# Threshold attention and a feed-forward block: raw weight chunks with other limits, fewer begun behind the turning, additions behind the thresholds

## The chip, the core and the metric

One Trainium2 chip, of which the kernel uses one core. The metric is the device time of one execution in microseconds, lower is better. Profile times are counted from the first instruction of one profiled execution.

## What is computed

```python
def _attn_ref(q, k, v, tau):                       # q, k, v: (8, 8, 576, 64)
    scores = scale * np.matmul(q, k.transpose(0, 1, 3, 2))
    thresh = np.max(scores, axis=-1, keepdims=True) - tau
    scores = np.where(scores >= thresh, scores, -1000000000.0)
    scores = scores - np.max(scores, axis=-1, keepdims=True)
    attn = np.exp(scores)
    attn = attn / (np.sum(attn, axis=-1, keepdims=True) + 1e-09)
    return np.matmul(attn, v)

def _moe_ref(x, g_ln, w_ch1, w_ch2):               # x: (8, 576, 512), heads side by side
    mu = np.mean(x, axis=-1, keepdims=True)
    var = np.mean((x - mu) ** 2, axis=-1, keepdims=True)
    xn = (x - mu) / np.sqrt(var + 1e-06) * g_ln
    return x + np.maximum(xn @ w_ch1, 0.0) @ w_ch2
```

`w_ch1` (512 x 2048) and `w_ch2` (2048 x 512) come in as 64-bit floats. The kernel sees them as 64-bit integers and makes 32-bit floats of them itself.

## The kernel before

**Slots.** The attention of one batch is cut into nine slots (`SLOTS = 9`), 72 in all. A slot takes two heads and half of their rows, or, in the fifth, the remaining rows of all heads. In the main loop, a slot `n` goes through these steps: `scores` (L402) on TensorE; `exponentials`, with the row maximum (L416) on VectorE, the threshold (L420) on GpSimd and the exponential (L429) on ScalarE; `weights`, which masks and sums (L436) on VectorE and divides by the sum (L452) on GpSimd; and the turning of the weights. From slot 6 on (`FIRST = 6`), the turning is `turn_blocks` (L520, L526): VectorE transposes blocks into `et`, a DMA writes `et` to a scratch in DRAM (`scr`), and in the next slot `fetch` reads it back as `em` and `er`. The products with v (`values_of`, L595 and L605) then run at the end of the next slot. Each slot has four quarters, at whose ends `second_part(n, i)` gives TensorE a share of the feed-forward work.

**The feed-forward.** It is done in sixteen groups of 288 tokens. Group 0 begins in slot 6, group 1 in the middle of slot 10. `first_part` makes 64 products with `w_ch1`, each followed after four by a Relu on ScalarE (L793) into `hidden`. Group 0 (`plain`) then makes 64 products with `w_ch2` in `second_plain`; later groups use `second_quarters`. A product of 288 columns is four records in the trace. Two PSUM banks (`ps_ff`) take turns, so a product can wait for the Relu that frees its bank. The planner asks before each product whether the chunk of weights is there (`conversion.carried`), and gives none of it if not.

The variance's inverse root is refined by three VectorE instructions (`root`, L734 to L738). Their scratch is `sq[:, 2]` and `sq[:, 3]`, which are the last two blocks of `hidden`; so `first_part` runs `root` (the line `while d == ND - 2 and len(rooted) <= g`) before it writes those blocks.

**The weights.** The class `Weights` turns 32 chunks of 128 x 512 (16 of each matrix) from 64 to 32 bits:

- `fetch` (L259): SyncE issues the DMA of a raw chunk, 512 KB, into a free piece of some other tile. `piece` takes, of the pieces whose limit is above the chunk's number, that with the lowest limit.
- `prepare_to`: ScalarE takes the absolute value of the high words (L275) and later scales the low words (L280).
- `begin` (L290, L293, L297): three VectorE instructions on the high words.
- `carry` (L305, and L308 for `w_ch1`): GpSimd adds the low words, and the piece is free again.

`begin_to(most)` begins chunks up to a number; `carry_all` carries all that are begun, the latest first; `convert` is both. The numbers for each slot stand in `BEGUN`: how many chunks are begun at the masks (`masks_at`), behind the masks (`behind_at`) and at the slot's end behind the turning (`end_at`). In each engine's queue, instructions stand in the order in which this code issues them. SyncE's queue also carries the loads of q, k, v, the writes to `scr` and the reads of `em`.

**Pieces.** The destination of the second matrix, `w2_sb`, lends eight pieces. Each is the home of two chunks, 16 + 2p and 17 + 2p, so a raw chunk must have left before its home is written. `hidden`, `et`, one buffer of `x`, one of `sq`, `stage` and, from slot 6, `e_room[1]` lend the others.

Of the kernel before, what the change touches and what calls it, by code (L numbers as in the profile page):

```python
# [8 lines left out]
F32 = mybir.dt.float32  # L9
# [4 lines left out]
AF = mybir.ActivationFunctionType  # L14
# [4 lines left out]
def kernel(  # L19
# [31 lines left out]
    nc = tc.nc  # L51
# [6 lines left out]
    ND = DF // 128  # L58
# [4 lines left out]
    SLOTS = 2 * HP + 1  # L63
# [10 lines left out]
    ffn = ctx.enter_context(tc.tile_pool(name="ffn", bufs=2))  # L74
# [6 lines left out]
    eps_sb = consts.tile([128, 1], F32, name="eps_sb")  # L81
# [93 lines left out]
    WC = 512  # L175

    class Weights:
# [13 lines left out]
        def __init__(self):  # L191
            self.chunks = [
                (w1_sb[i][:, c : c + WC], w_ch1[i * 128 : (i + 1) * 128, c : c + WC], i)
                for c in range(0, DF, WC)
                for i in range(NK)
            ] + [
                (
                    w2_sb[:, m, d : d + 4].rearrange("p d c -> p (d c)"),
                    w_ch2[d * 128 : (d + 4) * 128, m * 128 : (m + 1) * 128].rearrange(
                        "(d p) c -> p d c", p=128  # L200
                    ),
                    None,
                )
                for m in range(NK)
                for d in range(0, ND, 4)
            ]
            self.n1 = NK * (DF // WC)
            self.fetched = self.prepared = self.converted = self.begun = self.carried = 0
            self.raw, self.ticks = {}, 2
            flat = lambda t: t.rearrange("p a b -> p (a b)")  # L210

            x_room = ffn.tile([128, NK, TOK], F32, tag="x", bufs=3, name="x_room")
            y_room = ffn.tile([128, NK, TOK], F32, tag="sq", bufs=1, name="y_room")
            et_room = att.tile([128, NB, 128], F32, tag="et", bufs=1, name="et_room")
            stage = self.stage = consts.tile([128, 8, WC], F32, name="stage")

            n1 = self.n1  # L220
            self.free = []
            for t, n, before in (
                (w2_sb.rearrange("p m d c -> p (m d) c"), ND // 2, lambda p: n1 + 2 * p - 6),
                (hidden, 4, lambda p: 10),
                (x_room, 1, lambda p: 2 * n1),
                (y_room, 1, lambda p: 2 * n1),
                (et_room, 2, lambda p: n1 - 3),
                (stage, 4, lambda p: 2 * n1),
            ):
                for p in range(n):  # L230
                    self.free.append((before(p), -1, flat(t)[:, p * 2 * WC : (p + 1) * 2 * WC]))

        def take(self, t):
            t = t.rearrange("p a b -> p (a b)")
            for p in range(2):
                self.free.append((2 * self.n1, -1, t[:, p * 2 * WC : (p + 1) * 2 * WC]))

        def piece(self, i, wait):

# [21 lines left out]
                )  # L261

        def give(self, got):
            self.free.append((got[0], self.ticks, got[2]))

        def words(self, i, t):
            return self.raw[i][2].bitcast(t).rearrange("p (n two) -> p n two", two=2)
# [1 line left out]
        def prepare_to(self, most, lows=True):  # L269

            new = range(self.prepared, max(self.prepared, min(most, self.fetched)))
            for i in new:
                assert all(self.raw[j][0] + 6 > i or self.raw[j][0] == 10 for j in range(self.carried, i))
                dst, top = self.chunks[i][0], self.words(i, F32)[:, :, 1]
                nc.scalar.activation(dst, top, func=AF.Abs)  # L275
            self.prepared = max(self.prepared, min(most, self.fetched))
            while self.converted < (self.prepared if lows else self.begun):
                low, low_in = self.words(self.converted, I32), self.words(self.converted, U32)
                self.converted += 1
                nc.scalar.activation(  # L280
                    low[:, :, 0], low_in[:, :, 0], func=AF.Copy, scale=2.0**-29
                )
# [43 lines left out]
    FIRST = HP + 2  # L326
# [404 lines left out]
    def root(y, x, t):  # L731


        nc.vector.scalar_tensor_tensor(  # L734
            out=t, in0=y, scalar=-0.5, in1=y, op0=ALU.mult, op1=ALU.mult
        )
        nc.vector.tensor_mul(t, t, x)
        nc.vector.scalar_tensor_tensor(out=y, in0=t, scalar=1.5, in1=y, op0=ALU.add, op1=ALU.mult)  # L738
        rooted.append(y)
# [33 lines left out]
    def first_part(g):  # L773


        xc = centred.pop(g)
        rb = sq = None
        plain = g == 0
        sums_of = differences() if g == 1 else iter(())
        for d in range(ND):  # L780
            while conversion.carried < 4 * (d // 4 + 1):
                yield 0, 0
            while d == ND - 2 and len(rooted) <= g:
                run_all(aside)
            p1 = ps_ff.tile([128, TOK], F32, tag="ff", name="p1")
            for c in range(NK):
                product(
                    p1, lhsT=w1_sb[c][:, d * 128 : (d + 1) * 128], rhs=xc[:, c],
                    start=(c == 0), stop=(c == NK - 1),
                )  # L790
                if c < NK - 1:
                    yield 1, 1
            nc.scalar.activation(hidden[:, d], p1, func=AF.Relu)  # L793
            next(sums_of, None)
            yield 2, 1
            if sq is None and d and (part > 1 or d == ND // 2 - 1):
                squared = d
                sq = hidden[:, ND - NK :]
                nc.scalar.activation(sq, xc, func=AF.Square)
                for c in range(1, NK):  # L800
                    nc.gpsimd.tensor_tensor(out=sq[:, 0], in0=sq[:, 0], in1=sq[:, c], op=ALU.add)
            elif sq is not None and rb is None and (
                d >= squared + (7 if plain else 3) and part > (0 if plain else 1)
                or d == ND - NK - 1
            ):
                var = ps_ff.tile([128, TOK], F32, tag="ff", name="var")
                product(var, lhsT=avg_sb, rhs=sq[:, 0], start=True, stop=True)
                rb = ffn.tile([128, TOK], F32, tag="rb", bufs=2, name="rb")
                nc.scalar.activation(sq[:, 2], var, func=AF.Identity, bias=eps_sb)
                nc.scalar.activation(rb, sq[:, 2], func=AF.Ln)  # L810
                nc.scalar.activation(rb, rb, func=AF.Exp, scale=-0.5)
                aside.append(lambda: root(rb, sq[:, 2], sq[:, 3]))
                yield 1, 1
        for _ in sums_of:
            pass
        return rb
# [171 lines left out]
    def run(n, i):  # L988
        for fn, args in later_calls.pop((n, i), ()):
            fn(*args)  # L990
# [51 lines left out]
    else:  # L1042
# [10 lines left out]

    BEGUN = [
        (0, 0, 1), (2, 2, 3), (4, 4, 5), (6, 6, 7), (8, 8, 9), (10, 10, 11),
        (13, 16, 19), (21, 23, 24), (26, 27, 29), (31, 32, 32), (32, 32, 32),
    ]

    def constants(times):
# [5 lines left out]
    def plain_at(n):  # L1065

        return FIRST <= n <= SLOTS + 1

    def convert(to):
        conversion.begin_to(to)  # L1070
# [7 lines left out]
    for n in range(NS):  # L1078
# [9 lines left out]
            scale_q(n + 1, loaded[n + 1][0])  # L1088
        rest = exponentials(n)
        es, thr = next(rest)  # L1090
        run(n, 0)
        if n == HP + 2:
            next(rest, None)
        if n >= HP:
            conversion.fetch(3, -1 if n > FIRST else 1)
        run_first(stores)
        if n == FIRST:
            convert(masks_at)
        second_part(n, 0)
        while drops and drops[0][0] is nc.gpsimd:  # L1100
# [9 lines left out]
            conversion.fetch(2 if n else 1)  # L1110
        if n < SLOTS + HP:
            run_all(aside)
        if n != FIRST:
            convert(masks_at)
        if n < FIRST:
            conversion.prepare_to(end_at)
# [16 lines left out]
            conversion.carry_all()  # L1133
        box = []
        if blocks_go:
            conversion.fetch(3, wait=0)
            conversion.prepare_to(end_at, False)
            scr = turn_blocks(b, s, es)
            if n == FIRST:
                conversion.take(e_room[1])  # L1140
                conversion.fetch(2)
            conversion.carry_all()
            at_quarter(n + 1, 0, lambda b=b, s=s, scr=scr, box=box: box.append(fetch(b, s, scr)))
        else:

            made = turn_weights(s, es, diags)
            for i, at in enumerate(
                (-1, -1, 0, 0)
            ):
                if i == 3 and n + 1 == FIRST:  # L1150
                    at_quarter(n + 1, 0, conversion.prepare_to, BEGUN[n + 1][0], False)
                if i < 3:
                    at_quarter(n + 1, at, next, made)
                else:
                    at_quarter(n + 1, at, lambda made=made, box=box: box.append(next(made)))
# [17 lines left out]
            conversion.prepare_to(BEGUN[n + 1][0] - (n == FIRST - 1))  # L1173
        second_part(n, 3)
        conversion.begin_to(end_at)
        conversion.carry_all()
        if FIRST <= n < SLOTS:
            conversion.prepare_to(BEGUN[n + 1][0], False)
        if not plain_at(n):
# [42 lines left out]
```

## Time and profile before

| | us |
|---|---|
| median of 3 runs (1348.24 to 1349.08) | 1348.75 |
| the profiled execution | 1348.64 |
| its span | 1346.9 |
| busy in the span: TensorE, VectorE, GpSimd, ScalarE | 1315.2, 873.9, 624.9, 458.8 |
| chunks begun (L290) up to | 157 |
| slots 6, 7, 8, 9, 10, 11 begin (scores) at | 70.57, 96.56, 117.55, 138.23, 164.51, 182.59 |

A line of the timeline gives the start, the length, the engine, the line of the code, the operation, what it writes and reads, how many records are merged, and in brackets the idle time before it with the event that ended it. A line of the windows gives the stretch, its length, the busy time of TensorE's matmuls, of its weight loads, of VectorE, ScalarE and GpSimd, the granted share of TensorE's clock, the busy share of the DMA engines and the GB/s that they moved. SPq is SyncE's queue, whose instructions issue DMAs.

### The profile page before, as it was taken

The page shows a single profiled execution, that of the slowest core. Times are in us where ns is not written, and L with a number is a line of the kernel's source. Part 1 is how long each engine was busy: PE and PEld are TensorE (multiplying, and loading weights), DVE is VectorE, ACT ScalarE, POOL GpSimd, SP SyncE. Part 2 cuts the span into 40 slices and gives each one's busy share as a digit, 9 for nine tenths or more (in the row PEclk, how much of TensorE's full clock was granted, in tenths as well). Part 3 has the DMA queues.
Part 4 walks back from the last instruction along what each step waited for, and adds up shares of the span by engine and source line. Part 5 has one row for each costly group of instructions (what it writes and reads, how often), then busy time and mean ns, then how long its engine had stood idle before and what let it go on. Part 6 is the DMA issues. An engine that isn't in the chain of part 4 may idle for free.

```text
span 1346.9 us, 40264 instructions
## 1 busy us (share of the span) xinstructions
PE 1315.2 (98%) x17304; PEld 990.6 (74%) x17304; DVE 873.9 (65%) x1544; ACT 458.8 (34%) x995; POOL 624.9 (46%) x836
## 2 busy tenths in 40 slices
PE   8898899999999999999999999999999999999997
PEld 7665557769686786968778696877869677786957
DVE  7899786667666675666756677556756667666112
ACT  5875233232423233232233324233232323323120
POOL 3567456535444444444534454443444445335313
PEclk9999899999999999999999999999999999999999
DMA  8927864557643775447644576447754376443211
GB/s 164 302 75 202 207 176 163 178 150 193 179 150 120 193 200 159 151 156 192 172 149 151 166 179 191 142 143 193 197 171 151 121 199 180 133 156 124 85 19 20
DMA packets 335298, 213.92 MB, mean 159 GB/s; under 512 B 247376, under 2 KB 292688, under 8 KB 327056
## 3 DMA queue, kind: packets, MB, share of 16 engines
q1 hardware_dynamic: 329008, 210.46, 54.5%
q8 instruction: 136, 2.23, 0.7%
q10 hardware_dynamic: 5952, 0.74, 0.4%
q14 instruction: 42, 0.34, 0.1%
q0 software_dynamic: 160, 0.15, 0.1%
HBM read 124.00 MB, written 87.29 MB: 157 GB/s over the span
## 4 chain that ended last, share of the span: by engine, by line
PE 89%; DVE 4%; ACT 2%; DMA 2%; SPq 1%; issue 1%; POOL 1%; ACTq 0%; POOLq 0%; DVEq 0%
PE p L101 36%; PE seg L101 31%; PE sc L402 10%; PE sc L595 8%; PE sc L605 2%; ACT e L429 1%; DVE e L436 1%; PE tp L101 1%; SPq L118 1%; DVE w L297 1%; PE var L101 1%; PE mean L101 1%; DVE neg L416 0%; DMA em<-scr 0%; DVE w L293 0%
## 5 line engine op out<-in xcount | busy, mean ns | idle before, releaser
L101 PE MATMUL p<-xc,w 128*64 128x288 f32 x4096 | 518.9, 409 | 8.4 <-ACT part L880 4.6
L101 PEld LDWEIGHTS p<-xc,w 128*64 128x64 f32 x4096 | 287.4, 137 | 217.8 <-issue 14.9
L416 DVE TENSOR_REDUCE neg<-sc 128x2 f32<-128x1152 f32 x144 | 188.8, 1352 | 286.1 <-PE sc L402 285.6
L452 POOL TENSOR_SCALAR e<-e,den 128x576 f32<-128x576 f32 x264 | 205.8, 792 | 131.3 <-DVE den L441 131.3
L101 PE MATMUL seg<-hidden,w 128*64 128x144 f32 x3840 | 247.9, 287 | 0.0
L101 PEld LDWEIGHTS seg<-hidden,w 128*64 128x64 f32 x3840 | 234.8, 137 | 11.5 <-issue 8.5
L436 DVE SCALAR_TENSOR_TENSOR e<-sc,thr,e 128x576 f32<-128x576 f32 x288 | 222.5, 810 | 19.2 <-POOL thr L420 11.6
L420 POOL TENSOR_SCALAR thr<-neg,low_sb 128x2 f32<-128x2 f32 x144 | 40.3, 280 | 382.6 <-DVE neg L416 381.6
L793 ACT ACTIVATE hidden<-p 128x288 f32<-128x288 f32 x256 | 106.5, 416 | 303.3 <-PE p L101 302.2
L429 ACT ACTIVATE e<-sc,neg 128x576 f32<-128x576 f32 x288 | 197.4, 753 | 2.4 <-DVE neg L416 2.4
L526 DVE STREAM_TRANSPOSE et<-e 128x1152 f32<-128x1152 f32 x118 | 161.0, 1372 | 14.2 <-POOL e L452 13.7
L402 PE MATMUL sc<-kT,qT 64*64 64x384 f32 (+3 forms) x2048 | 140.3, 404 | 2.5 <-DVE e L436 1.6
L595 PE MATMUL sc<-em,v_in 128*64 128x128 f32 (+1 forms) x2368 | 131.5, 265 | 5.9 <-DMA em<-scr 2.8
L595 PEld LDWEIGHTS sc<-em,v_in 128*64 128x64 f32 x2368 | 124.1, 138 | 14.5 <-DVE w L297 3.0
L101 PE MATMUL seg<-hidden,stage 128*64 128x144 f32 x1920 | 123.3, 287 | 0.0
L101 PEld LDWEIGHTS seg<-hidden,stage 128*64 128x64 f32 x1920 | 117.6, 137 | 2.9 <-issue 2.9
L618 ACT COPY x<-sc 128x128 f32<-128x128 f32 x120 | 31.6, 265 | 247.2 <-PE sc L402 175.9
L865 POOL TENSOR_TENSOR hidden<-hidden 128x576 f32<-128x576 f32 x60 | 84.8, 1428 | 52.0 <-ACT hidden L793 42.4
L402 PEld LDWEIGHTS sc<-kT,qT 64*64 64x64 f32 x2048 | 76.3, 133 | 44.1 <-issue 21.3
L880 ACT COPY part<-seg 128x288 f32<-128x288 f32 x74 | 29.8, 403 | 190.6 <-PE seg L101 190.1
L865 DVE TENSOR_TENSOR hidden<-hidden 128x576 f32<-128x576 f32 x60 | 51.2, 887 | 51.5 <-PE seg L101 48.5
L101 PE MATMUL seg<-hidden,e 128*64 128x144 f32 x896 | 61.2, 286 | 0.0
(125 smaller groups left out, 1048.0 us busy)
## 6 DMA issues: line engine op xcount, KB each, us to landing
scr<-et SPq DMA_DIRECT2D x63, 1152.0 KB, 5.0
em<-scr SPq DMA_DIRECT2D x63, 1024.0 KB, 5.8
out_dram<-ot SPq DMA_DIRECT2D x248, 36.0 KB, 3.7
q_in<-in_q_dram SPq DMA_DIRECT2D x120, 72.0 KB, 2.8
er<-scr SPq DMA_DIRECT2D x132, 64.0 KB, 5.1
k_in<-in_k_dram SPq DMA_DIRECT2D x116, 72.0 KB, 3.0
v_in<-in_v_dram SPq DMA_DIRECT2D x28, 256.0 KB, 5.5
w<-in_moe_w_ch_dram SPq DMA_DIRECT2D x10, 512.0 KB, 8.3
```

The costliest lines, as they stand in the source:

```text
L101: nc.tensor.matmul(out[r], lhsT=lhsT[:, r], rhs=rhs, **flags)
L402: nc.tensor.matmul(sc[h][64 * i : 64 * i + 64, at : at + n], lhsT=ql[r] if s == HP else qT[r, half, j * 128 + 64 * i : j * 128 + 64 * i + 64],
L416: nc.vector.tensor_reduce(out=neg[:, i], in_=pairs[h], axis=AXL.X, op=ALU.max, negate=True,)
L420: nc.gpsimd.tensor_scalar(out=thr[:, i], in0=neg[:, i], scalar1=-1.0, scalar2=low_sb, op0=ALU.mult, op1=ALU.add,)
L429: nc.scalar.activation(es[:, i], blocks[i], func=AF.Exp, bias=neg[:, i : i + 1])
L436: nc.vector.scalar_tensor_tensor(out=es[:, i], in0=blocks[i], scalar=thr[:, i : i + 1], in1=es[:, i], op0=ALU.is_ge, op1=ALU.mult, accum_o ...
L452: nc.gpsimd.tensor_scalar(out=es[:, i], in0=es[:, i], scalar1=den[:, i : i + 1], scalar2=1.0, op0=ALU.mult, op1=ALU.mult,)
L526: nc.vector.transpose(et[:, :, 64 * h : 64 * h + 64].rearrange("p n (j c) -> p j n c", j=2), es[:, 2 * h : 2 * h + 2].rearrange("p j (n c) ...
L595: nc.tensor.matmul(dst[64 * h : 64 * h + 64], lhsT=vt[:, h, c, :], rhs=pick(em[:, 2 * j : 2 * j + 2, c], h), start=c == 0 and first, stop= ...
L618: nc.scalar.copy(x_of(2 * b + (s > HP))[:, s % (HP + 1), 128 * j : 128 * j + 128], pv[j])
L793: nc.scalar.activation(hidden[:, d], p1, func=AF.Relu)
L865: eng.tensor_tensor(out=out[at], in0=in0[at], in1=in1[at], op=op)
```

## The change

It touches the planning of the raw chunks, the scratch of the root and where chunks are begun and carried in slots 6 to 10.

```diff
-    (w2_sb.rearrange("p m d c -> p (m d) c"), ND // 2, lambda p: n1 + 2 * p - 6),
+    (w2_sb.rearrange("p m d c -> p (m d) c"), ND // 2, lambda p: (16, 16, 19, 21, 24, 24, 25, 29)[p]),
...
+                    home = 99 if t.shape[-1] != 128 or n != ND // 2 else n1 + 2 * p
...
-                assert all(self.raw[j][0] + 6 > i or self.raw[j][0] == 10 for j in range(self.carried, i))
+                assert all(self.raw[j][3] > i for j in range(self.carried, i))
...
-            while d == ND - 2 and len(rooted) <= g:
+            while d == ND - 2 and len(rooted) <= g and not plain:
                 run_all(aside)
...
-                nc.scalar.activation(sq[:, 2], var, func=AF.Identity, bias=eps_sb)
-                nc.scalar.activation(rb, sq[:, 2], func=AF.Ln)
+                two = [sq[:, c] for c in (2, 3)]
+                if plain:
+                    two = [ffn.tile([128, HM, HT], F32, tag="part", bufs=4, name="two") for _ in two]
+                    two = [t.rearrange("p m t -> p (m t)") for t in two]
+                nc.scalar.activation(two[0], var, func=AF.Identity, bias=eps_sb)
+                nc.scalar.activation(rb, two[0], func=AF.Ln)
                 nc.scalar.activation(rb, rb, func=AF.Exp, scale=-0.5)
-                aside.append(lambda: root(rb, sq[:, 2], sq[:, 3]))
+                aside.append(lambda: root(rb, *two))
...
     BEGUN = [
         (0, 0, 1), (2, 2, 3), (4, 4, 5), (6, 6, 7), (8, 8, 9), (10, 10, 11),
-        (13, 16, 19), (21, 23, 24), (26, 27, 29), (31, 32, 32), (32, 32, 32),
+        (13, 16, 16), (19, 21, 21), (24, 25, 27), (29, 30, 31), (32, 32, 32),
     ]
...
+    def early_at(n):
+
+        return n == FIRST or n == SLOTS + 1
...
         es, thr = next(rest)
+        conversion.carry_all()
         run(n, 0)
...
         if n >= HP:
-            conversion.fetch(3, -1 if n > FIRST else 1)
+            conversion.fetch(1 if n == FIRST + 2 else 3, -1 if n > FIRST else 1)
         run_first(stores)
-        if n == FIRST:
+        if early_at(n):
             convert(masks_at)
         second_part(n, 0)
...
-        if n != FIRST:
+        if not early_at(n):
             convert(masks_at)
...
         if blocks_go:
-            conversion.fetch(3, wait=0)
+            conversion.fetch(0 if n == FIRST + 2 else 3, wait=0)
             conversion.prepare_to(end_at, False)
             scr = turn_blocks(b, s, es)
             if n == FIRST:
                 conversion.take(e_room[1])
-                conversion.fetch(2)
+            if n == FIRST:
+                conversion.fetch(3)
             conversion.carry_all()
...
         second_part(n, 3)
         conversion.begin_to(end_at)
-        conversion.carry_all()
+        if n < FIRST:
+            conversion.carry_all()
+        conversion.prepare_to(0, False)
```

The limits of the eight pieces of `w2_sb` become a list of their own, and each piece now carries its home's number for the assertion. In slots 6 and 7, `behind_at` equals `end_at`, so nothing is begun after the turning; all chunks from 16 on are begun later, the last one in slot 10, where it stands ahead of the first quarter's products. What is begun at the end of slots 8 and 9 is carried in the next slot, behind the thresholds of that slot. In slot 8 one raw chunk is fetched at the most. Group 0's root gets two tiles of the tag `part` as scratch, and no longer has to be done before the last blocks of `hidden` are written.

## The prediction

> **What bounds the kernel now.** I read the page first (TensorE busy 98% of the span, so at most some 31 us of its idle time can be won), then the TensorE timeline around the slots that the change touches, then the windows of those slots, then VectorE, SyncE and GpSimd in the same stretch. Slots 6 to 10 begin with their `scores` (L402) at 70.57, 96.56, 117.55, 138.23 and 164.51 us. TensorE, slots 7 to 10 (start, length, what, and in brackets the idle time before and its releaser):
>
> ```profile
> 105.32 3.73 PE L101 MATMUL p<-xc,w 128*64 128x288 f32 x16 [2.60 <-ACT hidden L793]
> ...
> 124.91 8.47 PE L101 MATMUL p<-hidden,w 128*64 128x288 f32 x68 [1.21 <-POOL q_in L335]
> ...
> 134.34 1.75 PE L595 MATMUL sc<-em,v_in 128*64 128x128 f32 x28 [0.75 <-DVE w L293]
> ...
> 154.95 0.44 PE L595 MATMUL sc<-em,v_in 128*64 128x128 f32 x4 [2.33 <-DVE o L707]
> 158.23 3.26 PE L595 MATMUL sc<-em,v_in 128*64 128x128 f32 x28 [2.84 <-DMA em<-scr]
> ```
>
> Idle 2.60 + 1.21 + 0.75 + 2.33 + 2.84 = 9.7 us, and 0.54 us before the next group's first product at 174.60. The windows (length, then busy time by engine, then granted clock) show a second price:
>
> ```profile
> 105.13:108.54 3.41, 3.22 (x14) 1.72 (x16) 3.27 (x6) 3.41 (x8) 2.87 (x4) 0.50 1.16 293
> ...
> 156.33:163.15 6.82, 4.92 (x36) 4.12 (x38) 3.46 (x3) 0.00 (x0) 2.81 (x3) 0.50 0.92 184
> ```
>
> Half the clock costs half of 3.41 = 1.7 us, and half of what was worked after 158.23 (4.9 us) = 2.5 us. So all that can be won here is 9.7 + 0.5 + 4.2 = 14.4 us; after 175 us TensorE runs back to back and a gain made here is kept to the end.
>
> Why it waits: VectorE is full (third busy figure of a slot), then SyncE's queue is.
>
> ```profile
> 96.56:117.55 20.99, 18.36 (x180) 10.65 (x176) 20.51 (x31) 13.52 (x28) 18.32 (x17) 0.92 0.83 225
> 117.55:138.23 20.68, 18.72 (x196) 12.46 (x192) 20.27 (x36) 11.88 (x23) 12.97 (x14) 1.00 0.74 205
> ```
>
> ```profile
> 100.47 1.66 DVE L297 SCALAR_TENSOR_TENSOR w<-x_room,w 128x512 uint32<-128x512 uint32 x1
> 102.05 2.61 DVE L416 TENSOR_REDUCE neg<-sc 128x2 f32<-128x1152 f32 x2
> ```
>
> ```profile
> 131.24 1.67 SPq L259 DMA_DIRECT2D stage<-in_moe_w_ch_dram x3
> 133.01 5.79 SPq L118 DMA_DIRECT2D q_in<-in_q_dram x4
> 138.85 3.98 SPq L118 DMA_DIRECT2D k_in<-in_k_dram x4
> 142.93 4.07 SPq L533 DMA_DIRECT2D scr<-et x4
> ```
>
> Scores of slot 7 were done at 98.68, but the maximum (L416) began at 102.05, behind the three chunks begun after the turning of slot 6; exponentials and then a Relu that frees a bank hang on it (the 2.60). In slot 8 the turned weights were ready at 137.92 (L526) but left only at 142.93, behind three raw chunks and eight loads; their return (`em`) landed at 158.10 (the 2.84). "DVE w L293" and "DVE o L707" had nothing to do with the other two waits: the `em` quarters landed at 134.2 and 154.8.
>
> **What the Trainium skill says.** "SBUF — State Buffer", Who interferes with whom: a VectorE instruction with two SBUF inputs, or in a two-port mode, excludes GpSimd and is excluded by it. The trace agrees: a begun chunk (L290, L293, L297) takes 1.5 us alone (126.62 to 128.10) and 2.4 us beside GpSimd (112.41 to 114.79), while L436, one of whose inputs is in PSUM, takes 0.81 us in both. "TensorE: Matmul & The Clock Gate", What's actually happening: half clock follows an idle window of about 3.4 us. Here the low stretches are 3.41 and 6.82 us long, but idle sums of 2.60 and 5.2 us sufficed; the measurement decides.
>
> **The change part by part.**
>
> *Order on TensorE.* Second products need chunk 16 + k/4 carried (added up). Carried at a slot's quarters 0, 1, 3: slot 7 16, 19, 21; slot 8 21, 24, 25; slot 9 27, 29, 30; slot 10 32. The trace needs 21 second products by the end of slot 8, 46 before the values of slot 9, 50 by its end: allowed are 36, 52, 56. So the products stay in their quarters; only waits change.
>
> *Pieces.* Following the free list, 26 chunks instead of 24 are fetched before slot 6, two more transfers behind 66 us where SP next works at 93.88: free. Slot 7 loses its three transfers, slot 8 has one for three, slot 9 gets the last three (29 to 31) behind its `em`.
>
> *No chunk begun behind the turning.* Turning 6 ends at 93.8 as before; VectorE then waits for the scores: maximum 98.65 to 101.2 instead of 102.05 to 104.6. The Relu comes before TensorE is through its eight products (102.7): 2.60 + 1.7 us go. `em` of slot 6 lands at 110.8 in the trace, TensorE would want it at 109.7: 0.9 back. Scores 8 end at 116.2 instead of 119.6.
>
> VectorE then carries the chain: maximum 2.53 and et 2.55 (starts 102.05, 104.58, 116.66, 119.21), four weights with reciprocals 3.35 (109.06 to 112.41), begun chunk 1.5 or 2.4.
> - Slot 7: 101.2 + three begun 4.5 + weights 3.35 + two begun beside GpSimd 4.3 = 113.4; turning to 116.0 (before: 119.3).
> - Slot 8: maximum to 118.5; the q scaling on GpSimd 1.4 and q transposes to 120.9; root 1.8 (moved behind the transposes; with its own scratch no Relu waits for it, so the 1.21 go); three begun to 127.2; weights to 130.6; one begun 133.0; GpSimd first makes three additions (3 x 1.29 = 3.9), then four divisions (3.7) to 134.8; turning to 136.1 (before 137.9).
> - Slot 9: two begun to 139.2; maximum to 141.7; then thresholds, and behind them two additions to 144.7 and only then the q scaling, 145.4: k transposed early, q waits 3 us. Transposes and o to 146.6, two begun 149.8, weights 153.1, o and ot 154.2, chunk 29 156.5, turning 159.1, chunk 30 160.6.
> - Slot 10: the maximum can start at 160.6.
>
> *Values.* From turning to the last landing of `em` took 15 us twice (119.3 to 134.2; 142.9 from SP's start to 158.1). Slot 7's: 131 against a TensorE that is there at 128.6: a wait of 2.0 (0.75 before). Slot 8's: SP takes 5.8 us for the eight loads without chunks (154.41 to 160.2) and 9.9 with three; with one about 7, done at 135.5, ready for the turning at 136.1: landed 151.3 instead of 158.1.
>
> *Additions behind thresholds.* Chunk 27 is the second of two additions after 149.8: done 152.4. TensorE wants it (the 24th of 25 products, 0.49 each, since 48 records, four to a product, take 5.97 us; from 137.1) at 148.5: a new wait of 3.9, likely with 1.7 of low clock. Then two products, values 1.75, four products: scores 10 from 159.1 to 161.1 (before 164.51 to 166.6). Maximum to 163.6, threshold, addition of chunk 30 to 165.2; TensorE, after six products at 164.1, waits 1.1. Chunk 31, begun 164.5, added 167.3, product 60 at 167.7. Last eight products with mean and the copy of L831: group 1 begins at 170.4 instead of 174.60.
>
> Sum: 4.2 us. Against the ideal 14.4, the new waits take 0.9 + 2.0 + 3.9 + 1.1 + 0.5 + 1.7 = 10.1. The profiled execution took 1348.64 us (span 1346.9 and 1.7 around it), 0.1 from the median 1348.75. Forecast: 1344.6 us.
>
> Unknowns with ends: begun beside GpSimd 1.5 or 2.4 (four such, 3.6 us together; I take 2.1 to 2.4, measured); low clock in slot 9 0 or 1.7 (I take 1.7); eight loads 5.8 or 9.9 (I take 7); landing of a raw chunk 5.3 (the first at 131.24) to 10.9 (x_room at 54.79), I take 5.3, because only `em` lies ahead.
>
> **Rivals.**
> 1. *TensorE bound.* If chunks go at 1.5 and GpSimd delays less, the maximum of slot 10 is ready when scores 10 are, and only the `em` wait of 2 and small change stay: 14.4 - 5.4 = 9 us, 1339.6. For: TensorE work from scores 7 to scores 10 needs only 68.0 - 9.7 - 4.2 = 54 of the 68.0 us between their starts. Against: summed VectorE work from 98.65 is 60 us, with GpSimd waits 62 to 65.
> 2. *The wait only moves.* Begun chunks have merely gone from slots 6 to 9 into 8 to 10, and VectorE stands unused 93.8 to 98.65. If its chain is 3 us longer than I sum: 1347.6. For: turning 9 ends at 159.1 in my sum, 159.7 in the trace of before.
> 3. *Slower: chunk 29 lands late.* It was fetched at 131.24, and is now issued near 148 behind `em`; chunk 29 stands on VectorE ahead of turning 9, maximum 10 and the addition of chunk 30. It costs nothing until it lands past 153.6. With the 10.9 us seen at 54.79, and 2.7 for loads that take 9.9: landing 161.6, 8 us late; 1344.6 + 8 = 1352.6. It decides against the change from about 4 us late. Against: the last three such transfers behind an `em` took 5.3 to 7.5.
>
> **How the numbers follow.** Forecast 0.42 (1343 to 1347), rival 1 0.2, rival 2 0.16, rival 3 and its like 0.22. No change is within 0.2%, 2.7 us: 1346.05 to 1351.45. Faster 0.34 + 0.2 = 0.54; the same 0.08 + 0.14 = 0.22; slower 0.24 with rival 2's tail. Range 1338.5 to 1352; the likeliest alone 1343 to 1347.
>
> **What would show it.** Maximum of slot 7 right at the end of its scores and the 2.60 gone; no wait before 124.9's product; turning 8 near 136; SP starting slot 8's scr with it; new waits of TensorE on GpSimd L305 in slots 9 and 10; group 1's first product near 170.4. Wrong if raw chunk 29 is what VectorE waits for (rival 3), or if TensorE waits for nothing but `em` (rival 1).

## The result and the profile after

| | before | after |
|---|---|---|
| median of 20 runs each, us | 1349.12 (1347.64 to 1350.38) | 1347.01 (1345.22 to 1348.12) |
| the profiled execution, us | 1348.64 | 1347.32 |
| its span, us | 1346.9 | 1345.5 |
| slot 6's scores go on at, us | 70.57 | 71.64 |
| group 1's first product, us | 174.60 | 173.13 |
| from the one to the other, us | 104.03 | 101.49 |

The ratio after to before is 0.9984, with a 95% interval of 0.9978 to 0.9991: some 2.1 us faster, where 4.2 us was predicted. The profiled execution of after reached slot 6 1.07 us late. The change does alter the order of fetches up to there, but the ten experiments below that fetch in the same order reached slot 6 at 70.61 to 70.93 us, so most of the 1.07 belongs to that one execution. So every time of after that is set against the prediction is taken less 1.07, and the last row of the table is what the change did in that execution: 2.54 us.

The timeline of TensorE after, same stretch and same columns as before:

```profile
107.77 4.59 PE L101 MATMUL p<-xc,w 128*64 128x288 f32 x36 [0.64 <-ACT hidden L796]
...
121.74 8.41 PE L101 MATMUL p<-hidden,w 128*64 128x288 f32 x68
...
132.83 1.75 PE L598 MATMUL sc<-em,v_in 128*64 128x128 f32 x28 [2.35 <-DVE w L293]
...
154.21 1.75 PE L101 MATMUL p<-hidden,w 128*64 128x288 f32 x8 [4.07 <-POOL w L308]
155.73 3.09 PE L598 MATMUL sc<-em,v_in 128*64 128x128 f32 x32
...
167.42 1.68 PE L101 MATMUL p<-hidden,w 128*64 128x288 f32 x12 [1.28 <-POOL w L308]
...
170.31 2.16 PE L101 MATMUL p<-hidden,w 128*64 128x288 f32 x16 [0.25 <-POOL w L308]
173.13 4.59 PE L101 MATMUL p<-xc,w 128*64 128x288 f32 x36 [0.66 <-DVE xc L673]
```

The 2.60 and the 1.21 of before are gone (0.71 and 0.64 stand where the 2.60 stood), and so are the 2.33 and 2.84 ahead of slot 9's values. In their place stand a longer wait for `em` in slot 8 (the label names VectorE, but the last quarter of `em` landed at 132.69) and four waits on GpSimd's additions and what stands behind them. The windows of after show slots 7 and 8 and the one low stretch of the clock (before there was one of 3.41 and one of 6.82):

```profile
97.63:115.76 18.13, 16.78 (x181) 10.03 (x177) 15.56 (x28) 12.31 (x26) 11.16 (x13) 1.00 0.68 173
115.76:136.72 20.96, 18.61 (x197) 11.43 (x193) 20.01 (x35) 12.65 (x24) 12.52 (x14) 1.00 0.77 172
154.71:158.12 3.41, 3.41 (x30) 2.88 (x28) 3.34 (x6) 1.95 (x3) 3.41 (x5) 0.50 1.09 227
```

Slot 7 is 2.9 us shorter; slot 8 keeps its length (0.3 more) and its full VectorE (20.01 of 20.96). Idle time is now 0.71 + 0.64 + 2.35 + 4.07 + 1.28 + 0.25 + 0.66 = 9.96 us, and the low clock costs half of 3.41, 1.7 us: 11.7 us against 14.4 before. The difference, 2.7, is the 2.54 of the table to 0.2 us.

SyncE's queue in slot 8, where its order was changed:

```profile
129.40 0.53 SPq L262 DMA_DIRECT2D w<-in_moe_w_ch_dram  x1
130.03 3.86 SPq L118 DMA_DIRECT2D q_in<-in_q_dram  x4
133.94 3.29 SPq L118 DMA_DIRECT2D k_in<-in_k_dram  x4
137.54 3.83 SPq L536 DMA_DIRECT2D scr<-et  x4
```

Behind one raw chunk the eight loads take 7.2 us (9.8 behind three), and `scr` leaves at 137.54, with the end of the turning (137.52) and no longer 5 us after it.

### The profile page after: what moved, and what is told of

The parts are those of the page before. It is cut to its first block, busy times and chain, and to the rows that moved or that the text cites. A ratio compares the mean times of both kernels' runs of the same rounds, so it can differ in the third digit from the quotient of the medians.

```text
span 1345.5 us, 40255 instructions
## 1 busy us (share of the span) xinstructions
PE 1313.5 (98%) x17304; PEld 989.7 (74%) x17304; DVE 870.6 (65%) x1544; ACT 458.7 (34%) x995; POOL 621.9 (46%) x836
## 4 chain that ended last, share of the span: by engine, by line
PE 91%; ACT 3%; DVE 2%; DMA 1%; POOL 1%; issue 1%; SPq 1%; POOLq 0%; ACTq 0%; DVEq 0%
PE p L101 38%; PE seg L101 31%; PE sc L405 10%; PE sc L598 9%; PE sc L608 2%; ACT e L432 1%; PE tp L101 1%; DVE e L439 1%; POOL w L308 1%; PE var L101 1%; PE mean L101 1%; SPq L118 0%; DMA scr<-et 0%; ACT em L489 0%; DMA k_in<-in_k_dram 0%
```

## The experiments

All changes are against the changed kernel, but for the one that says otherwise. The last column is from slot 6's scores to group 1's first product in the one profiled execution, as in the table above; it contains that execution's low clock, which differs from one execution to the next (last section).

| | median, us | ratio to before (95%) | stretch, us |
|---|---|---|---|
| before | 1349.12 | | 104.03 |
| the change | 1347.01 | 0.9984 (0.9978 to 0.9991) | 101.49 |
| additions at the slot's end | 1344.71 | 0.9974 (0.9965 to 0.9984) | 99.66 |
| additions oldest first | 1350.49 | 1.0015 (1.0008 to 1.0023) | 105.41 |
| root's scratch in `sq` | 1346.91 | 0.9983 (0.9975 to 0.9991) | 102.11 |
| one chunk behind slot 6's turning | 1347.66 | 0.9994 (0.9986 to 1.0002) | 102.31 |
| kernel before, new `BEGUN` alone | 1351.99 | 1.0022 (1.0015 to 1.0029) | 107.54 |
| v loaded behind `em` | 1346.43 | 0.9981 (0.9972 to 0.999) | 101.50 |

**Additions at the slot's end.** In the prediction's working, the carrying behind the thresholds costs a q wait of 3 and makes the wait for chunk 27. This puts it back where the kernel before had it:

```diff
         es, thr = next(rest)
-        conversion.carry_all()
         run(n, 0)
...
-        if n < FIRST:
-            conversion.carry_all()
-        conversion.prepare_to(0, False)
+        conversion.carry_all()
```

> The changed kernel, but what is begun at the end of slots 8 and 9 is added at once on GpSimd, ahead of the next slot's thresholds, as before the change. Theory V (VectorE's chain bounds slots 7 to 10, and the additions behind the thresholds hold up its q scaling by 2.97 us in slot 9 and chunk 30 until 167.4 in slot 10): q waits for 1.5 us less or not at all, TensorE's wait of 1.28 for the addition in slot 10 goes; 1.5 to 2.5 us faster than the changed kernel, about 1345. Theory P (the place behind the thresholds is a gain of the change, since thresholds come earlier): slower by 1 to 2.6 us, about 1348.5. Theory D (the way of the turned weights through DRAM bounds): within 0.5 us.

Measured 1344.71 us, 2.3 us better than the change by the medians, 1.3 by the ratios (the two intervals just overlap; the stretch is 1.8 us shorter, and of the four kernels below that add to this one and keep latest first, three lie at 1344.9 to 1345.4). GpSimd of the changed kernel, where slot 9's two additions stand between the thresholds and the q scaling (L338):

```profile
143.19 0.27 POOL L423 TENSOR_SCALAR thr<-neg,low_sb 128x2 f32<-128x2 f32 x1 [0.21 <-DMA scr<-et]
143.42 1.30 POOL L308 TENSOR_TENSOR w<-w,e 128x512 int32<-128x512 int32 x1
144.67 1.31 POOL L308 TENSOR_TENSOR w<-w,stage 128x512 int32<-128x512 int32 x1
145.96 0.74 POOL L338 TENSOR_SCALAR q_in<-q_in,scl_sb 128x576 f32<-128x576 f32 x1
```

and of this kernel, where they are done before the second threshold is due:

```profile
139.96 1.30 POOL L308 TENSOR_TENSOR w<-w,e 128x512 int32<-128x512 int32 x1 [3.31 <-issue]
141.22 1.29 POOL L308 TENSOR_TENSOR w<-w,stage 128x512 int32<-128x512 int32 x1
...
143.45 0.27 POOL L423 TENSOR_SCALAR thr<-neg,low_sb 128x2 f32<-128x2 f32 x1
143.70 0.74 POOL L338 TENSOR_SCALAR q_in<-q_in,scl_sb 128x576 f32<-128x576 f32 x1
```

Its VectorE and its TensorE show what follows from that:

```profile
144.47 0.77 DVE L360 STREAM_TRANSPOSE qT<-q_in 128x256 f32<-128x256 f32 x2 [1.43 <-POOL q_in L338]
...
154.97 1.05 DVE L293 TENSOR_SCALAR w<-w 128x512 f32<-128x512 f32 x1 [1.32 <-ACT w L278]
```

```profile
151.95 2.19 PE L101 MATMUL p<-hidden,w 128*64 128x288 f32 x8 [2.28 <-POOL w L308]
```

The q transposes wait 1.43 instead of 2.97, and TensorE 2.28 instead of 4.07 for chunk 27. But the earlier VectorE now meets a late transfer: ScalarE's L278 waits for the raw chunk 29, and VectorE 1.32 behind it. That is rival 3's mechanism, seen here and not in the changed kernel, where VectorE came to that chunk later than the data.

**Additions oldest first.** `carry_all` takes the latest chunk first, which lets TensorE wait for the older one, 27.

```diff
-            for i in reversed(range(self.carried, self.begun)):
+            for i in range(self.carried, self.begun):
```

> The changed kernel, with the additions of one call made in rising order of the chunks, so that chunk 27 comes before 28. Theory V: TensorE's wait of 4.07 us in slot 9 becomes 2.8, its low clock may go (1.7), but VectorE is free for the maximum of slot 10 only at 162.1, so 0.5 to 1.5 us faster, about 1346. Theory D: nothing.

It is slower, even than before: 1350.49 us. Two views of this kernel, VectorE and then GpSimd in slot 7, show why:

```profile
103.76 0.69 DVE L300 SCALAR_TENSOR_TENSOR w<-w 128x512 uint32<-128x512 uint32 x1
104.37 1.52 DVE L293 TENSOR_SCALAR w<-w 128x512 f32<-128x512 f32 x1
105.92 1.39 DVE L296 TENSOR_SCALAR w<-w 128x512 uint32<-128x512 uint32 x1
```

```profile
103.94 3.09 POOL L308 TENSOR_TENSOR w<-w 128x512 int32<-128x512 int32 x2 [2.07 <-ACT w L283]
```

Oldest first, GpSimd need not wait for the last of the three chunks: it adds the first two beside the third, whose L293 and L296 take 1.52 and 1.39 instead of 0.42 and 0.43. The same stands in slot 8 (L296 1.41 at 126.57, 1.40 at 129.08). Counted from slot 6's scores, turning 8 ends 2.9 us later than in the changed kernel. Latest first, the order itself holds GpSimd off until VectorE's run is over. This agrees with what the Trainium skill, "SBUF — State Buffer", Who interferes with whom, says of exclusion: of two instructions that need the ports shared by both engines, the second waits until the first is done.

**Root's scratch in `sq`.** The root has its scratch in blocks of `hidden` again and must be done before these are written.

```diff
-            while d == ND - 2 and len(rooted) <= g and not plain:
+            while d == ND - 2 and len(rooted) <= g:
...
-                if plain:
+                if False:
```

> The changed kernel with the root's scratch put back into hidden and the root again ahead of the last two blocks of hidden. Theory V: TensorE's wait of about 1.1 us at the start of slot 8 returns, but VectorE does the same work before the begun chunks of slot 8 in another order, and slot 9's maximum does not come later: 0 to 0.5 us slower than the changed kernel. If waits of TensorE add up wherever they are: 1.2 us slower.

Measured 1346.91 us, no difference from the change. In its profile TensorE has no wait from 106.82 to 129.78, where the 1.21 of before stood ahead of these products:

```profile
121.09 8.47 PE L101 MATMUL p<-hidden,w 128*64 128x288 f32 x68
```

With the earlier VectorE the root is in time anyway. This part of the change is worth nothing in this place.

**One chunk behind slot 6's turning.** VectorE stands unused 4.87 us ahead of slot 7's maximum. Here it begins chunk 16 there.

```diff
-        (13, 16, 16), (19, 21, 21), ...
+        (13, 16, 17), (19, 21, 21), ...
...
-            conversion.prepare_to(end_at, False)
+            conversion.prepare_to(end_at if n > FIRST else behind_at, False)
```

> The changed kernel with one chunk, 16, begun behind the turning of slot 6, in the 4.87 us in which VectorE waits for the scores of slot 7. Theory V: every step of VectorE from the weights of slot 7 to the maximum of slot 10 is 1.5 us earlier, TensorE's wait for chunk 27 is 2.6 instead of 4.07, group 1 begins 1 to 1.5 us earlier: about 1345.7. Rival (the reason of the change holds to the last chunk: anything begun behind the turning of slot 6 delays the maximum of slot 7, and TensorE's wait of 2.6 returns): slower by 1 to 3 us. Theory D: as V in slot 8, since the turning of slot 7 is earlier too, but not more than 0.5 in the end.

Measured 1347.66 us, 0.65 worse than the change (the intervals overlap; a gain like the forecast one is not there). VectorE of this kernel:

```profile
97.68 1.21 DVE L293 TENSOR_SCALAR w<-w 128x512 f32<-128x512 f32 x1 [3.63 <-ACT w L278]
98.92 0.80 DVE L296 TENSOR_SCALAR w<-w 128x512 uint32<-128x512 uint32 x1
99.76 0.69 DVE L300 SCALAR_TENSOR_TENSOR w<-w 128x512 uint32<-128x512 uint32 x1
100.37 2.62 DVE L419 TENSOR_REDUCE neg<-sc 128x2 f32<-128x1152 f32 x2
```

The chunk waits 3.63 us for ScalarE, whose L278 stands behind Relus that follow TensorE, and then takes 2.7 us beside GpSimd, and the maximum begins 1.5 us later than in the changed kernel, counted from slot 6's scores: most of the gap was not to be had. TensorE waits 0.75 more for a Relu (at 103.65), the scores of slot 8 come later by it, and VectorE waits 0.75 for them at 117.90.

**The kernel before with the new numbers alone.** Only `BEGUN` is changed; pieces, fetches, root and additions are those of before.

```diff
-        (13, 16, 19), (21, 23, 24), (26, 27, 29), (31, 32, 32), (32, 32, 32),
+        (13, 16, 16), (19, 21, 21), (24, 25, 27), (29, 30, 31), (32, 32, 32),
```

> The kernel before with the new numbers of begun chunks alone, so nothing behind the turning of slots 6 and 7, but with the old pieces: 24 chunks are fetched before slot 7 instead of 26, and five raw chunks stand on SyncE's queue in slot 8, three of them between the loads of q and k and the weights of slot 8. Theory V: VectorE's chain is the changed kernel's up to slot 8, then the weights of slot 8 leave 3 to 5 us late and TensorE waits for them in slot 9 as before the change; the gain is lost: 1348 to 1351. If the fetch plan is not needed for the gain: 1346 to 1347.5.

Measured 1351.99 us, 2.9 slower than before. SyncE's queue of this kernel:

```profile
140.45 1.67 SPq L259 DMA_DIRECT2D stage<-in_moe_w_ch_dram  x3
142.21 5.71 SPq L533 DMA_DIRECT2D scr<-et  x4
```

Three raw chunks and 10.7 us of loads still stand ahead of `scr`, and the last quarter of slot 8's `em` lands at 158.20; TensorE has 1.49 and 2.38 ahead of slot 9's values, where before had 2.33 and 2.84. To these come waits for additions, 2.84 in slot 9 and 3.38 in slot 10, and the clock is halved for 10.24 us from 151.16 on. So with the old pieces and fetches the new numbers are a loss.

The first experiment (1344.71) has the same numbers and the same place of the additions. It differs from this kernel in the pieces and fetches, in the root's scratch, and in the place where slot 10 begins its chunk. The root's scratch made no difference to the changed kernel; so, with the new numbers, the other two are worth some 7.3 us. They were not taken apart, and no run shows what the fetch plan is worth with the old numbers.

**v loaded behind `em`.** SyncE issues the v loads of slots 7 and 8 behind `em`, so that `em` leaves earlier.

```diff
-            load_v((n + 2) // SLOTS * HP + (n + 2) % SLOTS)
+            u = (n + 2) // SLOTS * HP + (n + 2) % SLOTS
+            if n in (SLOTS - 2, SLOTS - 1):
+                at_quarter(n + 1, 0, load_v, u)
+            else:
+                load_v(u)
```

> The changed kernel with the loads of v in slots 7 and 8 (three DMAs, 3.7 us on SyncE's queue) put behind the reading back of the weights. em of slots 7 and 8 can land 1 to 2 us earlier. Theory V: TensorE's wait of 2.35 us in slot 8 shrinks, but the maximum of slot 9 and all behind it hang on VectorE: no more than 0.5 us faster than the changed kernel. Theory D: 1 to 2 us faster.

Measured 1346.43 us, 0.6 less than the change; the two intervals overlap almost wholly. The wait in slot 8 falls from 2.35 to 1.22, and TensorE waits in slot 9 instead: a new 0.89 at 145.01 for the additions behind slot 9's thresholds, and 4.08 for chunk 27 as ever; the stretch is 101.50 against 101.49. `em` is not what sets the end of the stretch; the chain through VectorE and GpSimd is.

**Looking for more.** Four kernels add to the first experiment:

| added to "additions at the slot's end" | median, us | ratio to before (95%) |
|---|---|---|
| v loads of slots 7, 8 behind the next slot's loads of q and k | 1344.87 | 0.9974 (0.9964 to 0.9984) |
| last chunk begun at slot 9's end: `(29, 30, 32)` | 1347.3 | 0.9989 (0.9981 to 0.9997) |
| both of these | 1345.32 | 0.998 (0.9971 to 0.9989) |
| the last chunk, and two raw chunks fetched in slot 8 | 1345.38 | 0.997 (0.9958 to 0.9982) |

A fifth (oldest first, one chunk behind slot 6's turning, two raw chunks in slot 8) took 1346.26 us (0.9983, 0.9976 to 0.9989). In its slot 8, L296 takes 1.40 twice, as in the oldest-first kernel; what its other parts gain by themselves is not shown.

> The changed kernel with the additions at the slot's end, and the loads of v in slots 7 and 8 put behind the next slot's loads of q and k, so that em and raw chunks 29 to 31 are issued about 3 us earlier in slot 9. Theory V with landings as its next limit: the wait of 1.32 us of VectorE for chunk 29 goes, 0.8 to 1.5 us faster than 1344.7, about 1343.5. If the loads of v then hold up the weights of slot 8 instead: 1344.5 to 1346.

> The changed kernel with the additions at the slot's end and chunk 31 begun with chunk 30 behind the turning of slot 9; raw chunk 29 is fetched in slot 9 as in the changed kernel. Against the run with 1344.71: VectorE no longer waits for ScalarE ahead of chunk 31 (0.90) nor q for its addition (1.49), but the wait of 1.32 for chunk 29 to land stays and chunk 31 must land earlier than before. Theory V: 0.5 to 1.5 us faster, about 1343.7. If the landings of raw chunks now bind VectorE (as in the run with chunk 29 in slot 8, where VectorE waited 0.32 and 0.24 for them): no faster, 1344.7 or more.

> Both: additions at the slot's end, v behind q and k, chunk 31 begun with chunk 30. Theory V: 1.5 to 3 us faster than 1344.7, 1342 to 1343.

> The changed kernel with the additions at the slot's end (as in the run with 1344.71), chunk 31 begun with chunk 30 behind the turning of slot 9 instead of behind the maximum of slot 10, and raw chunk 29 fetched in slot 8. In the run with the additions at the end VectorE waited 1.32 us for chunk 29 to land, 0.90 for ScalarE ahead of chunk 31 and 1.49 for the q scaling behind its addition, and TensorE 1.52 for that addition. Theory V: these go, 1.5 to 3 us faster than 1344.7, 1342 to 1343. If one more begun chunk ahead of the maximum of slot 10 costs as much as it saves: 1344 to 1345.

> All three edits together, and raw chunk 29 fetched in slot 8 instead of slot 9, so that it does not land at 154.7 when VectorE wants it at 152. Theory V: the chain is 4 us earlier at the maximum of slot 10, and TensorE no longer waits for an addition in slot 9: 4 to 6 us faster than the changed kernel, 1341 to 1343. If the transfers bound (theory D), or one more raw chunk in slot 8 holds up the loads and the weights of slot 8 on SyncE's queue: at most 1 us faster, 1346 or more.

None is faster than the first experiment beyond the scatter, and two of the three kernels with `(29, 30, 32)` scatter more (1345.01 to 1348.72 and 1344.22 to 1348.07). In the third, with chunk 31 begun ahead of slot 10's maximum, GpSimd adds 31 and 30 together, the latest first. GpSimd and then TensorE of this kernel:

```profile
163.31 2.52 POOL L308 TENSOR_TENSOR w<-w,stage 128x512 int32<-128x512 int32 x2 [3.23 <-DVE w L300]
```

```profile
159.04 3.26 PE L101 MATMUL p<-hidden,w 128*64 128x288 f32 x24
165.88 2.01 PE L101 MATMUL p<-hidden,w 128*64 128x288 f32 x12 [3.59 <-POOL w L308]
```

Both additions are done at 165.83, and TensorE, though early, goes on at 165.88. In the fourth, with two raw chunks in slot 8, chunk 29 is ready but the loads hold `scr` again. SyncE of it:

```profile
129.75 7.14 SPq L118 DMA_DIRECT2D q_in<-in_q_dram  x4
136.94 2.64 SPq L118 DMA_DIRECT2D k_in<-in_k_dram  x4
139.67 4.69 SPq L536 DMA_DIRECT2D scr<-et  x4
```

`em` lands at 155.57, and TensorE waits 2.52 for it. So the best version is the first experiment, 1344.71 us against 1347.01 and 1349.12: the change with the additions left at the slot's end.

## Why the prediction was right, and where it was off

The measured 1347.0 us lies in the range, 2.4 above the forecast of 1344.6 and at the very end of the likeliest stretch. The direction and most of the waits and their places were right; the gain was half of what was predicted, and at 2.1 us it is less than the 2.7 that the prediction counts as no change, to which it gave 0.22. Against the prediction's list (measured times less 1.07):

- *Maximum of slot 7 with the end of its scores, the 2.60 and its low clock gone*: predicted 98.65, measured 98.71. The 0.9 expected for `em` did not come: it landed at 111.31 in the profile, ahead of its products at 112.19. Instead TensorE waits 0.71 and 0.64 for Relus. In ScalarE's queue they stand behind exponentials and behind its work on the three begun chunks (L283, 104.13 to 105.99), which the prediction left out.
- *No wait before 124.9's product*: the 1.21 is gone, but not for the reason given, the root's own scratch: the experiment without it has no wait there either. This was right by luck.
- *SyncE in slot 8*: eight loads "about 7", measured 7.2; turning 8 ends at 136.1 predicted and 136.4 measured, and `scr` leaves with it. The wait for slot 7's `em`: 2.0 predicted, 2.35 measured.
- *q waits 3 us behind two additions in slot 9*: measured 2.97. *A new wait of 3.9 for chunk 27, with 1.7 of low clock*: measured 4.07, with 1.7.
- *Chunk 30's addition*: a wait of 1.1, measured 1.28, at 166.3 instead of 165.2.
- *Group 1's first product*: predicted 170.4, measured 172.06. These 1.66 us are the miss within the stretch; another 0.4 is that the median of before was 1349.12 in these runs and not 1348.75, and the rest is what one profiled execution differs from a median.

The sum of new waits is 11.7 us instead of 10.1. The term that was too small is "begun beside GpSimd ... (I take 2.1 to 2.4)"; in the trace of before, one such chunk had already taken 2.95 (104.58 to 107.53, beside GpSimd's L305). VectorE of the changed kernel, behind slot 7's weights:

```profile
110.25 0.95 DVE L293 TENSOR_SCALAR w<-w 128x512 f32<-128x512 f32 x1
111.24 0.85 DVE L296 TENSOR_SCALAR w<-w 128x512 uint32<-128x512 uint32 x1
112.12 1.11 DVE L300 SCALAR_TENSOR_TENSOR w<-w 128x512 uint32<-128x512 uint32 x1
113.16 0.42 DVE L293 TENSOR_SCALAR w<-w 128x512 f32<-128x512 f32 x1
```

The first chunk takes 2.9 (110.25 to 113.16), the second 2.3 (to 115.44): together 5.2 for the 4.3 of the sum. Slot 8's single one takes 2.9 (131.76 to 134.69). Some of it comes back, because the transposes and the root were priced too high: by turning 8 the chain is only 0.3 late. Slot 9 has again 0.3 more for its two begun (3.5 for 3.2) and GpSimd begins its additions 0.2 later, so TensorE gets chunk 27 0.7 late.

At the scores of slot 10 the lateness is 0.8, and at the addition of chunk 30 it is 1.1. The last 0.5 is made behind that: TensorE waits 0.25 for chunk 31, for which the sum has no wait, and 0.66 for `xc`, where the sum has 0.5 for a copy. Both come from the step "Chunk 31, begun 164.5, added 167.3". It was added at 169.2:

```profile
166.62 1.02 DVE L293 TENSOR_SCALAR w<-w 128x512 f32<-128x512 f32 x1 [0.89 <-ACT w L278]
...
168.76 0.77 DVE L356 STREAM_TRANSPOSE kT<-k_in 128x576 f32<-128x576 f32 x1
171.02 0.77 DVE L360 STREAM_TRANSPOSE qT<-q_in 128x256 f32<-128x256 f32 x2 [1.50 <-POOL q_in L338]
...
172.54 1.54 DVE L673 TENSOR_TENSOR xc<-x,mean 128x288 f32<-128x288 f32 x4
```

VectorE first waits 0.89 for ScalarE (which has an exponential ahead of L278), then the chunk lies beside the addition of chunk 30 (1.02 for 0.42), and the q scaling stands behind its own addition, so q's transposes wait 1.50, and `xc`, for which group 1 waits, stands behind them. The prediction followed the additions to TensorE but not the q scaling behind them to `xc`. Of the 1.9 us by which chunk 31 is late, TensorE feels only these 0.4.

As to the rivals: TensorE alone is not the bound (rival 1), since it waits 4.07, 1.28 and 0.25 for GpSimd's additions in slots 9 and 10. Chunk 29 landed at 154.73 (less 1.07: 153.66, just at the point of 153.6 from which rival 3 counts): ScalarE had waited 8.68 us for it, VectorE not at all. Rival 2, the wait that only moves, is in part what happened: the chain is 1.66 us longer than summed, where it took 3.

## What to carry to other kernels

When work of one engine is moved behind a small result of another, list what stands behind it in its own queue: here two additions of 1.3 us delayed a q scaling and through it VectorE, and cost some 2 us. A gap on one engine is worth filling only if the feeding engine is ready in it (3.63 us of the 4.87 were ScalarE's), and the plan of transfers ahead of a critical read can decide whether a better order of instructions gains or loses (1344.71 against 1351.99). An order of additions that looks wasteful, latest first, can keep two engines off one another. And a wait of TensorE of 2 to 4 us should be priced with 1.7 us of half clock as a risk, as the next section shows.

## What the runs showed that was not expected

The low clock does not follow the wait's length alone. In two kernels of the last table, with the v loads later (the first has only this added, the third also the last chunk), TensorE waited in the same place, for the same chunk, at the same time. The first kernel's timeline of TensorE:

```profile
151.89 2.19 PE L101 MATMUL p<-hidden,w 128*64 128x288 f32 x8 [3.66 <-POOL w L308]
```

Its window from there (the clock is the third figure from the end):

```profile
151.89:155.30 3.41, 3.41 (x24) 2.44 (x26) 2.45 (x7) 0.68 (x1) 3.41 (x5) 0.53 1.12 314
```

The third kernel's timeline of TensorE:

```profile
151.91 1.19 PE L101 MATMUL p<-hidden,w 128*64 128x288 f32 x8 [3.67 <-POOL w L308]
```

Its window:

```profile
151.91:155.32 3.41, 3.41 (x46) 2.81 (x48) 2.90 (x7) 0.74 (x2) 3.41 (x5) 1.00 1.20 278
```

After 3.66 us the clock was halved, after 3.67 it was not, and twice as many records were done. In the first experiment 2.28 us were enough for half clock (0.51 from 151.95 to 155.36).

By the profiles, what decides is how a wait lies against windows that the clock keeps for itself. The Trainium skill, "TensorE: Matmul & The Clock Gate", What's actually happening, gives an idle window of about 3.4 us ahead of half clock and calls the window free-running, that is, not tied to the program. The traces agree with the length: in all 13 profiles, each stretch between two changes of the clock is a whole multiple of 3.413 us (before: 3.41 us low, then 47.79 full from 108.54 to 156.33, then 6.82 low). But they don't show that the whole window must be idle. If each profile is cut into windows of 3.413 us from its low stretch on, and TensorE's idle time is counted in each, then, from 60 us on, there are some 4800 windows at full clock. The 17 with 2.10 us of idle time or more were all followed by half clock; all others had 2.02 at most, and none of them was. Once the clock was low, less kept it low: 0.91 us and more in a window did (6 windows), 0.53 and less did not (17).

The third kernel's wait of 3.67 falls into two windows. Its later one of 3.59, shown further up at 165.88, falls mostly into one, and the window behind that is low:

```profile
146.61:150.02 3.41, 1.63 (x14) 0.72 (x10) 3.31 (x8) 0.00 (x0) 0.74 (x2) 1.00 0.95 248
150.02:153.43 3.41, 1.52 (x18) 1.12 (x20) 3.34 (x10) 0.12 (x1) 3.41 (x5) 1.00 0.99 332
...
163.68:167.09 3.41, 1.21 (x10) 0.77 (x12) 2.62 (x3) 2.71 (x5) 3.41 (x6) 1.00 0.89 250
167.09:170.50 3.41, 3.41 (x16) 1.71 (x14) 2.70 (x9) 0.10 (x1) 1.47 (x2) 0.50 0.86 256
```

TensorE's idle time is the length less the first busy figure: 1.78, 1.89 and 2.20 us. This is read from profiles; no run moved a wait to test it. By this count, as an estimate, a lone wait of under 2 us costs its length only, one of more than 4.2 always costs 1.7 us more, since half of it must lie in one window, and between them it depends on the execution. The ten times of the first experiment lie in two groups, seven at 1344.17 to 1344.94 and three at 1346.01 to 1346.37. Windows that lay otherwise would account for that, but only one of the ten was profiled.
